# Remainders of expert rooms on column groups in plain fp32, a last room of 32 tokens with unsplit weights, and another order of the visits

## The chip, the cores and the metric

The kernel runs on one core of a Trainium2 chip. The metric is the device time of one execution in microseconds. The engines are TensorE (PE, whose weight loads the profile lists as PEld), VectorE (DVE), ScalarE (ACT), GpSimd (POOL) and SyncE (SP), which issues most of the DMAs.

## The reference

The inputs are q, k and v of 8 batches, 8 heads, 576 positions and 64 channels, and the weights of a router and of 8 experts. All is fp32.

```python
# attention: causal, a window of 128 positions, ALiBi bias
scores = where(0 <= i - j < 128, q @ k.T / 8 - slope[h] * abs(i - j), -1e9)
attn = softmax(scores) @ v                      # -> x: 8 x 576 tokens of 512

# routing: a token may keep the expert of the token before it
logits = x @ w_gate
local = sigmoid(x @ w_local)
e[s] = argmax(logits[s]) if s == 0 or local[s] < 0.5 else e[s - 1]

# expert: 512 -> 1024 -> 512
out[s] = softmax(logits[s])[e[s]] * (relu(x[s] @ w1[e[s]]) @ w2[e[s]])
```

Each of the 4608 tokens goes to one expert. With these inputs the eight experts get 418, 646, 542, 577, 610, 416, 616 and 783 tokens, which can be counted from the reference.

## The kernel before

**Attention.** A pair of heads of one batch is a slot, 32 in all. Every engine's work is put out in an order written by hand (`FIRST`, `ORDER`, `LAST`): `S` scores on PE, `D` bias and minimum on DVE, `E` exponential on ACT, `N` normalising on POOL, `U` transposes, `M` weighted values and so on. Ahead of the first slot the constants are made: `make_bias` writes, for each of four head pairs, four tiles of ALiBi bias (pairs 0 and 1 on DVE, 2 and 3 on POOL), and `zero` clears the unused corners of the probability tiles of both buffers. `tokens` computes the router's logits of a batch, with 32-column weights whose four results lie in four column groups of one PSUM tile. Attention's result goes to a DRAM table `xd` by blocks of tokens.

**Rooms.** The experts' work is laid out in rooms of a fixed number of 32-token blocks (`_plan`). Experts 0, 1 and 2 have own rooms of 256, 384 and 512 tokens. What is left over of all experts is ranked by size on the chip, and rank r gets the rooms `RANKS[r]`. The visits are, in tokens: own 256, 384, 512, then 512, 288, 384, 256, 384, 256, 384, 224, 448, 288, 192 and 128. A token that finds no room is left for a loop behind everything (L1207), one pass for each 128 such tokens of an expert; it isn't entered when there are none.

**A visit** (`Fixed.run`). Weights and activations are split into two fp32r parts, high and low, and each product takes three matmuls (`three`, L969 to L971). The first layer has 8 hidden blocks of 128: for each, 4 x 3 matmuls with the room's tokens as columns. ReLU on ACT (L1014) and the low part on DVE (L1015) follow. The second layer takes tokens in windows of 128 (`windows`): 3 matmuls of 512 columns for each window and hidden block. Where the room isn't a multiple of 128 tokens, the last window is moved back so that it overlaps the one before, at full price. `finish` scales each window by the gate (L976 on DVE, L978 on ACT), and `scatter` (L963, POOL) writes its 128 rows to the output. The last room, of 128 tokens, is a `Flex` visit: its tokens are the weights of the first layer and its hidden values are transposed on PE.

**Supply.** `Stream` loads the weights in chunks of 512 KB, eight for each visit (`load`, up to 6 chunks ahead of the splitting), and splits each in halves: high part on ACT (L237), low part on DVE (L239); up to 6 split chunks are held. `Feed` collects the next room's tokens: gathers on POOL (L177), one for 32 tokens, with one for the gates of a window, then for each window `split_x`: transpose on DVE (L183), high part on ACT (L186), low part on DVE (L187). `tick` is called at set places of a visit, and puts out at most one such turn, one gather and, at every third tick, one scatter. A turn of the next room may come as soon as a visit begins. Scatters that are left when the visits end are issued one behind another. All engines keep the order in which their instructions are put out.

## Time and profile before

| | us |
|---|---|
| median of 3 runs | 694.97 (694.80 to 695.07) |
| profiled execution | 696.09 |
| its span, first to last instruction | 694.2 |
| PE busy | 675.5 (97%) |
| DVE busy | 481.8 (69%) |
| ACT busy | 424.4 (61%) |
| POOL busy | 390.7 (56%) |

The span is the time from the first to the last instruction; the rest of the execution's time lies around it. A busy share is an average over stages: attention to some 240 us, then the visits. Matmuls are pipelined, so the time from the start of one to the start of the next tells more of PE's price than the length of one. A "granted clock" of 1.00 is 2.4 GHz, and the lower level is 1.2 GHz. Line L162 is that of a helper through which attention's instructions pass.

### The profile page before, as it was taken

How to read it: one execution, taken by the hardware profiler on the slowest of the kernel's cores; microseconds unless marked ns; L12 is line 12 of the kernel's file. 1: busy time of each engine (PE TensorE's matmuls, PEld its weight loads, DVE VectorE, ACT ScalarE, POOL GpSimd, SP SyncE). 2: the span in 40 equal slices, each digit the busy share in tenths (PEclk: the TensorE clock that was granted, in tenths of full speed). 3: DMA queues.
4: the chain of work that ended last, by engine and by line, in shares of the span. 5: the costliest groups of instructions: out<-in, count | busy, mean ns of one | idle time of the engine just before them, and what ended most of it. 6: DMA issues, size and time to landing. Idle time of an engine off the chain costs nothing. (4 is left out here: it accounts for less than half of the span.)

```text
span 694.2 us, 16083 instructions
## 1 busy us (share of the span) xinstructions
PE 675.5 (97%) x5339; PEld 550.9 (79%) x5339; DVE 481.8 (69%) x1649; ACT 424.4 (61%) x1200; POOL 390.7 (56%) x659
## 2 busy tenths in 40 slices
PE   8999999999999989999999999999999999999995
PEld 4667767767766677888888989899989878889894
DVE  7579889889898999964633664665576477345572
ACT  5999999999988653543523553564555355344462
POOL 6866656656787727777771737447466475102311
PEclk9999999999999999999999999999999999999999
DMA  9845655655822966445454655576576566345550
GB/s 299 249 138 175 222 156 174 223 156 172 265 65 60 294 201 206 126 161 163 141 162 126 209 181 165 177 232 207 152 239 200 148 197 219 104 132 173 173 158 30
DMA packets 61254, 121.99 MB, mean 176 GB/s; under 512 B 9391, under 2 KB 28335, under 8 KB 61168
## 3 DMA queue, kind: packets, MB, share of 16 engines
q1 hardware_dynamic: 51248, 100.12, 45.8%
q0 software_dynamic: 9488, 20.22, 9.5%
q8 instruction: 43, 0.70, 0.4%
q10 hardware_dynamic: 432, 0.59, 0.3%
q14 instruction: 43, 0.35, 0.2%
HBM read 101.29 MB, written 20.20 MB: 175 GB/s over the span
## 5 line engine op out<-in xcount | busy, mean ns | idle before, releaser
L239 DVE TENSOR_TENSOR cut<-wraw,cut 128x512 fp32r<-128x512 f32 x231 | 150.3, 688 | 53.6 <-ACT cut L237 52.4
L177 POOL DMA_INDIRECT kr<-xd,xidx x141 | 152.7, 1083 | 55.9 <-issue 38.7
L237 ACT CAST cut<-wraw 128x512 fp32r<-128x512 f32 x212 | 120.7, 618 | 56.3 <-PE y L971 56.1
L971 PE MATMUL h<-qx,cut 128*128 128x384 f32 (+6 forms) x440 | 142.1, 323 | 0.0
L970 PE MATMUL h<-qx,cut 128*128 128x384 f32 (+6 forms) x440 | 141.9, 322 | 0.0
L969 PE MATMUL h<-qx,cut 128*128 128x384 f32 (+6 forms) x440 | 141.6, 322 | 0.0
L969 PE MATMUL y<-cut,hh 128*128 128x512 f32 x328 | 129.6, 395 | 1.9 <-ACT hh L1014 1.1
L971 PE MATMUL y<-cut,hl 128*128 128x512 f32 x328 | 129.0, 395 | 1.5 <-DVE hl L1015 1.4
L963 POOL DMA_INDIRECT out<-y,sidx x41 | 43.2, 1053 | 153.1 <-ACT y L978 118.8
L970 PE MATMUL y<-cut,hh 128*128 128x512 f32 x328 | 129.3, 394 | 0.0
L1014 ACT ACTIVATE hh<-h 128x384 fp32r<-128x384 f32 (+6 forms) x104 | 47.8, 460 | 127.7 <-PE h L971 127.7
L162 POOL TENSOR_SCALAR cut<-cut,r 128x192 f32<-128x192 f32 (+2 forms) x256 | 99.6, 407 | 44.4 <-DVE r L162 14.8
L162 ACT ACTIVATE cut<-scs,mn 128x192 f32<-128x192 f32 (+2 forms) x256 | 108.9, 429 | 8.3 <-DVE mn L162 7.9
L1015 DVE SCALAR_TENSOR_TENSOR hl<-h,hh 128x384 fp32r<-128x384 f32 (+6 forms) x112 | 56.7, 507 | 81.4 <-ACT hh L1014 80.6
L969 PEld LDWEIGHTS h<-qx,cut 128*128 128x128 f32 x440 | 83.6, 190 | 6.6
L970 PEld LDWEIGHTS h<-qx,cut 128*128 128x128 f32 x440 | 83.7, 190 | 6.4 <-DVE qx L187 0.2
L162 DVE CUSTOM_DVE_ANT_0 scs<-sc,bias 128x192 f32<-128x192 f32 (+2 forms) x288 | 83.2, 324 | 7.3 <-PE sc L162 4.4
L971 PEld LDWEIGHTS h<-qx,cut 128*128 128x128 f32 x440 | 83.7, 190 | 3.4 <-issue 0.4
L971 PEld LDWEIGHTS y<-cut,hl 128*128 128x128 f32 x328 | 61.7, 188 | 16.1 <-DVE hl L1015 3.1
L969 PEld LDWEIGHTS y<-cut,hh 128*128 128x128 f32 x328 | 61.9, 189 | 13.2 <-ACT hh L162 1.8
L970 PEld LDWEIGHTS y<-cut,hh 128*128 128x128 f32 x328 | 61.9, 189 | 10.4 <-DVE cut L162 0.2
L162 PE MATMUL pt<-ident,cut 128*128 128x128 f32 x448 | 69.8, 281 | 0.4
(222 smaller groups left out, 1006.2 us busy)
## 6 DMA issues: line engine op xcount, KB each, us to landing
wraw<-w SPq DMA_DIRECT2D x120, 512.0 KB, 4.6
kr<-kT SPq DMA_DIRECT2D x31, 288.0 KB
qx<-qT SPq DMA_DIRECT2D x30, 288.0 KB, 4.6
cut<-v SPq DMA_DIRECT2D x8, 1024.0 KB
xd<-T SPq DMA_DIRECT2D x8, 768.0 KB
xd<-T SPq DMA_DIRECT2D x8, 384.0 KB
kr<-xd,xidx POOLq DMA_INDIRECT x141, 3.7
v<-v SPq DMA_DIRECT2D x8, 128.0 KB
```

The source lines that it names most:

```text
L162: ins = getattr(self.engine, name)(*args, **kw)
L177: queued(nc.gpsimd.indirect_dma_start(out=r, out_offset=None, in_=src[0:n, :], in_offset=bass.IndirectOffsetOnAxis(ap=col, axis=0), bounds ...
L237: scalar.copy(c[:, 0, f], raw[:, f])
L239: (pool if 2 * n + f == POOL_CUT else vector).tensor_tensor(c[:, 1, f], raw[:, f], c[:, 0, f], ALU.subtract)
L963: queued(nc.gpsimd.indirect_dma_start(out=out[:, :], out_offset=bass.IndirectOffsetOnAxis(ap=col, axis=0), in_=y, in_offset=None, bounds_c ...
L969: nc.tensor.matmul(o, ah, bh, start=start, stop=False)
L970: nc.tensor.matmul(o, ah, bl, start=False, stop=False)
L971: nc.tensor.matmul(o, al, bh, start=False, stop=stop)
L1014: now.act.activation(hh, hp, AF.Relu)
L1015: nc.vector.scalar_tensor_tensor(hl, hp, 0.0, hh, ALU.max, ALU.subtract)
```

## The change

- The fifth rank's room has 416 tokens (448), the last rank's 32 (128). The rooms are visited in another order: own 256, 384, 512, then 512, 288, 384, 416, 256, 288, 384, 192, 256, 384, 224 and 32.
- A room whose last window would have 32 or 64 tokens (288 twice, 416, 192) no longer moves it back. For these tokens ReLU writes fp32 values (`hx`), the raw chunks of the second layer are kept in pairs of tiles, and `rests` multiplies in plain fp32: the tokens are 32 or 64 columns of weights, and the 512 outputs are cut in four or two pieces, one for each column group. It is put out once for two hidden blocks. Index, gate and scatter follow: a row of the output is scattered in four or two pieces.
- The last room is a `Mini`: both layers in plain fp32 on four column groups, with weights that aren't split. Its first layer is put out ahead of the last hidden block's second layer of the room before, its two transposes in the middle of that, and its second layer behind it.
- In attention's start, half of bias 0 and all of bias 1 are made on ACT, and the clears for the second buffer follow the first slot's last score (`D6`).

```diff
-RANKS = [(512, 288), (384, 256), (384, 256), (384, 224), (448,), (288,), (192,), (128,)]
+RANKS = [(512, 288), (384, 256), (384, 256), (384, 224), (416,), (288,), (192,), (32,)]
+ORDER_OF_ROOMS = [0, 1, 2, 8, 3, 9, 4, 10, 5, 6, 7, 11]
...
-    return own + left
+    return own + [left[i] for i in ORDER_OF_ROOMS]
...
 def windows(nb):
-    return [min(4 * t, nb - 4) for t in range((nb + 3) // 4)]
+    last = nb % 4
+    if last in (1, 2):
+        return [(t, 4) for t in range(0, nb - last, 4)] + [(nb - last, last)]
+    return [(min(4 * t, nb - 4), 4) for t in range((nb + 3) // 4)]
...
+                e, which, c, kind = self.order[self.n_raw]
+                if kind and which == ("b" if kind == "also" else "a"):
+                    if c % 2 == 0:
+                        self.pair = tp.tile([P, 2, 2, DM], F32, name="xT")
+                    t = self.pair[:, c % 2]
+                else:
+                    t = wr.tile([P, 2, DM], F32, name="wraw")
+                self.raw.append(load_chunk(e() if callable(e) else e, which, c, t))
...
+                if self.order[self.n_cut][3] == "only":
+                    self.cut[self.n_cut] = self.raw.pop(0)
+                    self.n_cut += 1
+                else:
+                    run(self.split(self.room(), now.act, nc.vector))
...
-        order += [(e if kind == "own" else by_rank[e], w, c) for w, c in (FLEX_ORDER if nb == 4 else FIXED_ORDER)]
+        keep = "only" if nb == 1 else "also" if nb % 4 in (1, 2) else None
+        order += [(e if kind == "own" else by_rank[e], w, c, keep) for w, c in (FLEX_ORDER if nb == 1 else FIXED_ORDER)]
...
+        def make_bias(p, *engines):

             for turned in range(2):
+                engine = engines[turned % len(engines)]
                 for c in range(2):
                     at = slice(64 * c, 64 * c + 64)
-                    engine.tensor_scalar(bias[at, turned, p], rel[at], -8.0 * 2.0 ** -(2 * p + (c ^ turned) + 1), 1.0, ALU.mult, ALU.mult)
+                    slope = -8.0 * 2.0 ** -(2 * p + (c ^ turned) + 1)
+                    if engine is act:
+                        act.activation(bias[at, turned, p], rel[at], AF.Copy, scale=slope)
+                    else:
+                        engine.tensor_scalar(bias[at, turned, p], rel[at], slope, 1.0, ALU.mult, ALU.mult)
...
         zero(*zero_p(0))
-        make_bias(0, dve)
-        make_bias(1, dve)
-        zero(*zero_p(1), V[0][1][64:128])
+        make_bias(0, dve, act)
+        make_bias(1, act)
...
+            yield
+            dve.tensor_scalar(piece[:, 0:1], roff, 1.0 / 32, None, ALU.mult)
+            dve.tensor_scalar(piece[:, 1:2], roff, 64.0, None, ALU.is_ge)
...
+                w, r = wins[lo]
+                if r < 4:
+                    dve.tensor_tensor(fw[:, lo].rearrange("p (a q) -> p a q", q=r), t[:, w:w + r].unsqueeze(1).broadcast_to([P, 4 // r, r]),
+                                      msel.rearrange("p (a q) -> p a q", q=r), ALU.mult)
+                else:
+                    while hi < n and wins[hi] == (wins[hi - 1][0] + 4, 4):
+                        hi += 1
+                    dve.tensor_tensor(fw[:, lo:hi], t[:, w:w + 4 * (hi - lo)].rearrange("p (c q) -> p c q", q=4),
+                                      msel.unsqueeze(1).broadcast_to([P, hi - lo, 4]), ALU.mult)
...
+            for c, (w, r) in enumerate(wins):
+                if r < 4:
+                    col = sc[:, c0 + c:c0 + c + 1]
+                    dve.tensor_scalar(col, col, 4.0 / r, piece[:, r - 1:r], ALU.mult, ALU.add)
+                    yield
...
+                if emitted[-1] == ("D6", 0):
+                    zero(*zero_p(1), V[0][1][64:128])
...
-        queued(nc.gpsimd.indirect_dma_start(out=out[:, :], out_offset=bass.IndirectOffsetOnAxis(ap=col, axis=0), in_=y, in_offset=None,
-                                            bounds_check=NTOK - 1, oob_is_err=False))
+        n = DM // y.shape[1]
+        queued(nc.gpsimd.indirect_dma_start(out=out.rearrange("t (a c) -> (t a) c", a=n), out_offset=bass.IndirectOffsetOnAxis(ap=col, axis=0),
+                                            in_=y, in_offset=None, bounds_check=n * NTOK - 1, oob_is_err=False))
...
-        y = mp.tile([P, DM], F32, name="y", bufs=4)
+        y = mp.tile([P, DM], F32, name="y", bufs=4)[:, :o.shape[1]]
...
+        def run(self, W, tick, mini=None, ready=None):
             N = 32 * self.rows.blocks
-            wins = [slice(32 * w, 32 * w + P) for w in windows(self.rows.blocks)]
-            n = len(wins)
-            ys = [py.tile([P, DM], F32, name="y") for _ in range(n)]
+            wins = windows(self.rows.blocks)
+            n, rest = len(wins), wins[-1][1] % 4
+            M = N - 32 * rest
+            ys = [py.tile([P, DM], F32, name="y")[:, :P * r] for _, r in wins]
             xh, xl = self.rows.xh[:, :, :N], self.rows.xl[:, :, :N]
-            hs = {}
-
-            def second(f):
+            hs, hx = {}, None
+
+            def second(f, then=()):
                 hh, hl = hs.pop(f)
-                vh, vl = W.at("b")
-                for t, sl in enumerate(wins):
-                    three(ys[t], hh[:, sl], hl[:, sl], vh[:, f % 2], vl[:, f % 2], f == 0, f == 7)
+                vh, vl, raw = W.at("b")
+                for t, (w, r) in enumerate(wins):
+                    if r == 4:
+                        sl = slice(32 * w, 32 * w + P)
+                        three(ys[t], hh[:, sl], hl[:, sl], vh[:, f % 2], vl[:, f % 2], f == 0, f == 7)
+                    elif f % 2:
+                        rests(ys[t], lambda ff: hx[:, ff % 2], raw, (f - 1, f), r)
                     if t == n // 2 - 1:
                         tick()
+                        for g in then:
+                            g()
                 if f % 2:
                     W.done("b")
...
-                hh = mp.tile([P, N], F32R, name="hh", bufs=3)
-                hl = mp.tile([P, N], F32R, name="hl", bufs=3)
-                now.act.activation(hh, hp, AF.Relu)
-                nc.vector.scalar_tensor_tensor(hl, hp, 0.0, hh, ALU.max, ALU.subtract)
+                hh = mp.tile([P, M], F32R, name="hh", bufs=3)
+                hl = mp.tile([P, M], F32R, name="hl", bufs=3)
+                now.act.activation(hh, hp[:, :M], AF.Relu)
+                nc.vector.scalar_tensor_tensor(hl, hp[:, :M], 0.0, hh, ALU.max, ALU.subtract)
                 hs[f] = (hh, hl)
+                if rest:
+                    if f % 2 == 0:
+                        hx_next = mp.tile([P, 2, 32 * rest], F32, name="hx")
+                    now.act.activation(hx_next[:, f % 2], hp[:, M:], AF.Relu)
                 if f % 2:
                     W.done("a")
                 tick()
                 if f > 0:
                     second(f - 1)
+                if rest and f % 2:
+                    hx = hx_next
                 tick()
-            second(7)
+            if mini:
+                ready()
+                mini.first(W)
+            second(7, [mini.turn] if mini else ())
             for t in range(n):
                 c = self.rows.t0 + t
                 finish(ys[t], self.rows.g[:, t:t + 1], self.rows.idx[2][:, c:c + 1], t % 2)
+
+    def rests(y, h, raw, fs, r):
+
+        for f in fs:
+            for g in range(4 // r):
+                o = slice(32 * r * g, 32 * r * g + 32 * r)
+                nc.tensor.matmul(y[o], h(f), raw[:, f % 2, P * r * g:P * r * g + P * r], start=f == 0, stop=f == 7, skip_group_check=True)
+
+    class Mini(Fixed):
+
+
+        def first(self, W):
+            raws = [W.at("a") if i == 0 else W.cut[W.find("a") + i] for i in range(4)]
+            hp = ph_.tile([P, 256], F32, name="h")
+            for kc in range(4):
+                for g in range(4):
+                    nc.tensor.matmul(hp[32 * g:32 * g + 32], self.rows.x[:, kc], raws[g][:, :, P * kc:P * kc + P], start=kc == 0, stop=kc == 3,
+                                     skip_group_check=True)
+            for _ in range(4):
+                W.done("a")
+            self.h = mp.tile([P, 256], F32, name="hl", bufs=3)
+            now.act.activation(self.h, hp, AF.Relu)
+
+        def turn(self):
+            pt = ptr.tile([P, 2, P], F32, name="tr")
+            for i in range(2):
+                pin(nc.tensor.transpose(pt[:, i], self.h[:, P * i:P * i + P], ident))
+            self.hT = mp.tile([P, 2, P], F32, name="hh", bufs=3)
+            now.act.copy(self.hT, pt)
+
+        def run(self, W, tick, *_):
+            y = py.tile([P, P], F32, name="y")
+            for g in range(4):
+                rests(y, lambda f: self.hT[:, f % 2, 32 * g:32 * g + 32], W.at("b"), (2 * g, 2 * g + 1), 1)
+                W.done("b")
+            c = self.rows.t0
+            finish(y, self.rows.g[:, 0:1], self.rows.idx[2][:, c:c + 1], 0)
+
+    class MiniRows(Rows):
+        def turn(self, t):
+            self.x = sh.tile([P, KS, 32], F32, name="qx")
+            pin(nc.vector.transpose(self.x.rearrange("p c i -> p (c i)"), self.r[:, 0, 0]))

...
-            visits.append(Flex(xidx[:, x:x + 4], ridx[:, c:c + 1], sidx[:, c:c + 1]) if nb == 4 else Fixed(Rows(x, c, nb, idxs)))
+            visits.append(Mini(MiniRows(x, c, nb, idxs)) if nb == 1 else Fixed(Rows(x, c, nb, idxs)))
...
         if isinstance(v, Fixed):
-            upto = i + 1
-            while upto < len(visits) and isinstance(visits[upto], Flex):
-                upto += 1
-            v.run(W, lambda: feed.tick(upto))
-            feed.finish(upto)
-        else:
-            v.run(W, lambda: feed.tick(upto, False))
+            mini = visits[i + 1] if i + 2 == len(visits) else None
+            v.run(W, lambda: feed.tick(i + 1), mini, lambda: feed.finish(i + 1))
+            feed.finish(i + 1)
```

## Rows read from the trace of the kernel before

**Rows 1.** The page, part 1: busy us of each engine, share of the span, instructions.

```profile
PE 675.5 (97%) x5339; PEld 550.9 (79%) x5339; DVE 481.8 (69%) x1649; ACT 424.4 (61%) x1200; POOL 390.7 (56%) x659
```

**Rows 2.** The table of stretches, one for a visit: those of 512 (own), 288, 384, 256, 224, 448, 192 and 128 tokens. Columns: the stretch in us, its length, then busy us and instructions of PE, PEld, DVE, ACT and POOL, the granted clock of PE as a share of 2.4 GHz, the DMA engines' share and GB/s.

```profile
294.11:337.72 43.61, 43.61 (x193) 35.97 (x192) 24.00 (x41) 17.29 (x31) 33.85 (x33) 1.00 0.51 161
...
381.24:410.58 29.34, 29.34 (x169) 26.18 (x168) 18.70 (x32) 14.71 (x29) 15.23 (x16) 1.00 0.59 187
410.58:443.99 33.41, 33.41 (x170) 30.31 (x168) 17.78 (x30) 14.82 (x28) 20.31 (x20) 1.00 0.57 176
443.99:466.63 22.64, 22.64 (x146) 20.43 (x144) 17.20 (x31) 14.27 (x29) 11.65 (x11) 1.00 0.71 219
...
556.11:582.18 26.07, 24.41 (x145) 21.26 (x144) 17.92 (x33) 14.48 (x30) 17.82 (x16) 0.93 0.64 201
582.18:623.61 41.43, 41.43 (x193) 36.07 (x192) 19.32 (x32) 15.71 (x30) 9.18 (x9) 1.00 0.45 139
...
652.95:674.66 21.71, 21.71 (x146) 19.73 (x144) 14.37 (x27) 12.79 (x27) 7.44 (x7) 1.00 0.61 186
674.66:686.30 11.64, 11.64 (x80) 10.63 (x79) 5.96 (x11) 5.89 (x13) 2.51 (x2) 1.00 0.11 42
```

**Rows 3.** The timeline of all engines in the first 22 us, its lines on the bias and the first scores. Columns: start us, us, engine, line, operation, tiles, form, count; in brackets the idle time before it and what ended it.

```profile
2.19 1.28 ACT L162 ACT_TABLE_LOAD   x1 [2.19 <-issue]
...
3.36 2.66 DVE L162 TENSOR_SCALAR bias<-rel 64x192 f32<-64x192 f32 x7 [1.06 <-POOL rel L162]
...
4.58 1.31 PE L162 MATMUL sc<-kr,qx 64*64 64x64 f32 x16
...
7.45 0.22 DVE L162 CUSTOM_DVE_ANT_0 scs<-sc,bias 128x64 f32<-128x64 f32 x1
...
7.71 0.35 ACT L162 ACTIVATE cut<-scs,mn 128x64 f32<-128x64 f32 x1 [4.24 <-DVE mn L162]
...
8.44 0.44 ACT L162 ACTIVATE cut<-scs,mn 128x192 f32<-128x192 f32 x1
```

**Rows 4.** The timeline of POOL from 580 us on: one of the gathers, and scatters of the last rooms.

```profile
586.84 1.00 POOL L177 DMA_INDIRECT kr<-xd,xidx  x1 [0.30 <-issue]
...
622.74 1.02 POOL L963 DMA_INDIRECT out<-y,sidx  x1 [29.21 <-ACT y L978]
626.31 1.00 POOL L963 DMA_INDIRECT out<-y,sidx  x1 [2.55 <-DVE cut L239]
630.99 0.98 POOL L963 DMA_INDIRECT out<-y,sidx  x1 [3.68 <-issue]
...
675.14 1.00 POOL L963 DMA_INDIRECT out<-y,sidx  x1 [8.61 <-ACT y L978]
679.47 1.51 POOL L963 DMA_INDIRECT out<-y,sidx  x1 [3.33 <-DMA out<-y,sidx]
687.79 0.98 POOL L963 DMA_INDIRECT out<-y,sidx  x1 [6.82 <-ACTq L1207]
```

**Rows 5.** The timeline of PE between 39.5 and 46 us, in the attention phase: `pt` are transposes, `pk<-xT,w` the router logits on four column groups, `xa` the weighted values on two column groups.

```profile
39.74 1.09 PE L162 MATMUL pt<-ident,cut 128*128 128x128 f32 x8
40.77 1.07 PE L162 MATMUL pk<-xT,w 128*32 128x512 f32 x8
41.76 0.98 PE L162 MATMUL sc<-kr,qx 64*64 64x192 f32 x20
42.68 0.65 PE L162 MATMUL xa<-pts,cut 128*64 128x256 f32 x4
43.26 0.43 PE L162 MATMUL pk<-xT,w 128*32 128x128 f32 x8
43.62 0.44 PE L162 MATMUL pt<-ident,cut 128*128 128x128 f32 x2
...
44.11 0.60 PE L162 MATMUL pt<-ident,cut 128*128 128x128 f32 x4
44.55 0.60 PE L162 MATMUL pk<-ident,part 128*128 128x128 f32 x4
```

**Rows 6.** The timeline of ACT in the visit of 224 tokens.

```profile
560.23 0.62 ACT L186 CAST qx<-xtr 128x512 fp32r<-128x512 f32 x1 [1.42 <-DVE xtr L183]
562.36 0.62 ACT L186 CAST qx<-xtr 128x512 fp32r<-128x512 f32 x1 [1.50 <-DVE xtr L183]
562.88 0.35 ACT L1014 ACTIVATE hh<-h 128x224 fp32r<-128x224 f32 x1
```

**Rows 7.** The groups of DVE by shape between 244 and 300 us (count | busy us, mean ns): the table of tokens, and one of the index operations.

```profile
L858 DVE TENSOR_SCALAR cw<-io,at_t 128x128 f16<-128x128 f16 x40 | 7.3, 289 | 0.0
...
L162 DVE TENSOR_SCALAR xidx<-fi,roff 128x128 int32<-128x128 f32 x1 | 0.3, 274 | 0.0
```

**Rows 8.** The timeline of PE in the same visit.

```profile
561.88 0.27 PE L971 MATMUL h<-qx,cut 128*128 128x224 f32 x1
563.28 0.50 PE L969 MATMUL y<-cut,hh 128*128 128x512 f32 x1 [1.13 <-ACT hh L1014]
563.62 0.40 PE L970 MATMUL y<-cut,hh 128*128 128x512 f32 x1
564.51 0.50 PE L971 MATMUL y<-cut,hl 128*128 128x512 f32 x1 [0.49 <-DVE hl L1015]
...
565.95 0.41 PE L971 MATMUL h<-qx,cut 128*128 128x224 f32 x1
```

More of the change, by code (lines that the diff above doesn't have):

```diff
@@ L224, in at_once, with load_chunk @@
             r.turn(t)
[L226 removed]
+    def load_chunk(e, which, c, t):
         src = w1 if which == "a" else w2
[L228 removed]
         if isinstance(e, int):
@@ L250, in load @@
             while self.n_raw < len(self.order) and self.n_raw < self.n_cut + RAWS:
-                e, which, c = self.order[self.n_raw]
-                self.raw.append(load_chunk(e() if callable(e) else e, which, c))
+                e, which, c, kind = self.order[self.n_raw]
[6 more added lines that the diff above has]
+                self.raw.append(load_chunk(e() if callable(e) else e, which, c, t))
                 self.n_raw += 1
@@ L257, in fill @@
                 self.load()
-                run(self.split(self.room(), now.act, nc.vector))
+                if self.order[self.n_cut][3] == "only":
[3 more added lines that the diff above has]
+                    run(self.split(self.room(), now.act, nc.vector))
             self.load()
@@ L266, in split @@
             raw = self.raw.pop(0)
-            self.cut[self.n_cut] = c[:, 0], c[:, 1]
+            self.cut[self.n_cut] = c[:, 0], c[:, 1], raw
             self.n_cut += 1
@@ L921, in rank_tables @@
         yield from fill_table(trk, a_t, PACE_TABLE)
-        yield from indices(trk, idxs, XO[0], TO[0], [at + w for kind, _, at, nb in PLAN if kind == "rank" for w in windows(nb)])
+        yield from indices(trk, idxs, XO[0], TO[0], [(at + w, r) for kind, _, at, nb in PLAN if kind == "rank" for w, r in windows(nb)])
         rank_done.append(1)
@@ L1219, in moe_attention @@
         at_once(v)
-        v.run(Stream([(ev, w, c) for w, c in FLEX_ORDER]), lambda: None)
+        v.run(Stream([(ev, w, c, None) for w, c in FLEX_ORDER]), lambda: None)
         scatter(*pending.pop())
```

15 lines of the change are left out of this document (4 added, 11 removed).

## The prediction

> **What bounds the kernel now.** I read the page first: the tensor engine is busy for 97% of the span, 675.5 of 694.2 us, and no other engine passes 70% [rows 1]. Busy shares of PE are lengthened by the pipeline, so the next view is the table of stretches, one for each visit to a room [rows 2]. There PE is busy through the whole of every visit but one; DVE has 14 to 24 us of work and ACT 13 to 17 in visits of 22 to 44 us. A visit therefore lasts as long as its columns stream, and prices follow from the table. The visit of 512 tokens has 96 first-layer and 96 second-layer matmuls, all of 512 columns: 43.61 / 192 = 0.227 us. With 0.227 for a second-layer matmul (3 for each window and hidden block), the first-layer matmul comes out at 0.204 us for 448 columns ((41.43 - 96 x 0.227) / 96), 0.178 for 384, 0.135 for 288, 0.122 for 256 and 0.113 for 192. The one visit with idle time on PE is that of 224 tokens: 24.41 of 26.07 us busy, clock 0.93.
>
> Two stretches are not bound by PE. At the start everything waits for DVE to make its constants [rows 3]. At the end three scatters run one after another [rows 4].
>
> **The rooms with a remainder.** Four rooms lose a window of the second layer: 288 tokens twice, 416 (was 448) and 192. A window is 3 matmuls for each of 8 hidden blocks: 24 x 0.227 = 5.45 us each. In its place, every second hidden block, stand plain fp32 matmuls on column groups. The kernel before has that very form: 32-column weights, four outputs in four column groups [rows 5]. Each fp32 matmul appears there twice (x8 for four), so I count two rounds for a group of four. Four of 512 columns take 41.76 - 40.77 = 0.99 us to the next start, four of 128 columns 43.62 - 43.26 = 0.36. The difference, 0.63 for 2 rounds of 384 more columns, is 0.105 us for a round of 128: the four groups stream together, or it would be four times that. The fixed part is 0.36 - 0.21 = 0.15 us, which includes leaving the mode; entering it costs another 0.15 (eight transposes ahead of it take 1.03, where four elsewhere take 0.44).
>
> With a remainder of 32, two hidden blocks take 4 rounds: 0.42 + 0.15 + 0.15 = 0.72 us, four times a room: 2.9. Bounds: 0.42 if the fixed parts hide, 0.87 if each group of four pays its 0.36 and the entry. I take 0.72, nearest to the row, with one entry and one exit. With a remainder of 64 there are two column groups and 256 columns; the nearest row is xa on 64-column weights: 0.58 us for two rounds with the exit, so 0.215 a round and 4 x 0.215 + 0.30 = 1.16 us, 4.6 a room (bounds 0.86 and 1.31). All of this is PE time on the path:
> - 288 tokens, twice: 2 x (-5.45 + 2.88) = -5.1
> - 416 tokens: -5.45 + 2.88, and 96 first-layer matmuls with 32 columns fewer, 0.191 for 0.204 (midway between the prices at 448 and 384): -1.3; together -3.9
> - 192 tokens: -5.45 + 4.64 = -0.8
>
> That is -9.8 us. The extra ReLU on ACT, eight in such a room, costs nothing: ACT has 14.7 of 29.3 us of work there [rows 2], and its reader comes after one or more windows of 0.68 us; uncovered, each is bounded by the 0.35 us of a 224-column ReLU [rows 6]. The raw chunks that are kept occupy two tiles, which the next room with a remainder asks for 16 chunks later, past the 12 chunks by which SP runs ahead, so SP isn't held. The extra index operations are a few DVE operations of up to 0.3 us [rows 7] in a visit where DVE works 24.0 of 43.6 us [rows 2].
>
> **The order of the visits.** No matmul is added or removed by it, and each room's eight loads and its gathers go with it. What changes is the neighbour. In the visit of 224 tokens the next room's four windows (448 tokens) are turned in its first two hidden blocks: three full ones and a half one, each a step on DVE, one on ACT (0.6 us) and one more on DVE, with ACT waiting 1.4 to 1.5 us for DVE before two of them [rows 6]. The ReLU stands behind these on ACT, so PE stops for 1.4 us from 561.88 and 0.9 from 563.62, and then it runs at the lower clock for a while: the same matmul lasts 0.41 us in place of 0.27 [rows 8], and the granted clock is 0.93 over the visit, between its levels of 1.2 and 2.4 GHz [rows 2]. A visit of 224 without this is 96 x 0.1175 (midway between 192 and 256) + 10.9 = 22.2 us, so 3.9 are lost. After the change this room's neighbour is the 32-token room, with one small transpose. Late next would be the other short rooms: before 288 (two windows and a 32-token one), 256 (two) and 384 (three). The visit of 256 at 444 us had three windows to turn and no idle PE (22.64 of 22.64). So -3.9, between 0 and -3.9.
>
> **The start.** Before, DVE makes eight pieces of bias (to 6.0 us) and clears ten tiles ahead of its first score at 7.45, so the clears take up to 1.4 us; the scores were on PE from 4.58 [rows 3]. Now it makes two pieces; ACT makes six, from the end of its table load at 3.47, at no more than the 0.44 of its 128x192 operation: to 6.1. The first exponential moves from 7.71 to about 6.1, and ACT is dense from there. The clears move behind the first pair's last score, where ACT has exponentials in hand. I take -1.5; bounds -2.4 (first score half a us after PE starts on them) and +1.4 (no gain, and the clears uncovered).
>
> **The end.** The last visit took PE 11.6 us, from 674.66 to 686.3 [rows 2]. The new one has a first part of 8 rounds of 256 columns, 8 x 0.215 + 0.3 = 2.0 us, and two transposes, 0.2, both ahead of the end of the 224-token room, then a second part of 16 rounds of 128: 2.0. On PE alone 11.6 become 4.2. But the room's two scatters and the last one are issued together at the end, and each waits for the landing of the one before: 675.14 to 679.47 is 4.33 us with a wait on that DMA, and three in a row stood 3.57 and 4.68 apart [rows 4]. Counted from the end of the last room's old position, the first scatter comes at 2.2 + 0.48 + 0.38 (the copy that ACT makes first) = 3.1, the third 8.7 later at 11.7, and the end 6.4 after that (687.79 to 694.2): 18.1 for 19.5, so -1.4. With spacings of 3.57 or 4.68: -2.9 or -0.7.
>
> **The sum.** -9.8 - 3.9 - 1.5 - 1.4 = -16.6 us. The profiled execution took 696.09 (span 694.2 and 1.9 around it), so 679.5; it lay 1.1 above the median of 694.97, and the forecast for the median is 678.4.
>
> **Rivals.**
> 1. The idle time moves to another short visit. For it: visits of 21 to 23 us have 14 to 17 us on DVE [rows 2], and the 192-token room now lasts some 20.9. Against: none has four windows to turn. Time: 678.4 + 3.9 = 682.3.
> 2. The start gives nothing, since a later wait swallows it: 679.9, or 681.3 with the clears uncovered.
> 3. The column groups overlap less beside these neighbours. By the row's upper bound (0.87 and 1.31) the rooms take 2.4 more and the last room's first part 0.5: 681.3. The Trainium skill, "TensorE: Matmul & The Clock Gate", Part 3 ("Measured speedup vs the span model"), gives 2.38 for three column tiles; an estimate by it stretches the streaming by 3 / 2.38, about 2.7 us more in all, 681.1. The trace leans against it: the 0.105 us of a round already holds all four groups [rows 5].
> 4. The scatters at the end don't wait for each other: the end follows PE, 2.2 + 2.0 + 1.5 (686.3 to 687.79) + 6.4 = 12.1 for 19.5, and the time is 672.4. Against: the waits of [rows 4].
> 5. Slower: the column groups run one after another. It decides where a pair of hidden blocks takes over 1.36 us in place of 0.72, for then a 288-token room gains nothing. Wholly serial, a pair takes 16 x 0.105 + 0.3 = 1.98 (+15.1 over twelve), with 64 tokens 2.02 (+3.4), and the last room's first part 7.2 (+5.2): 702.1. Against: the 0.36 of four groups [rows 5].
> 6. Slower: a room overflows. Counted from the reference's inputs, the fifth rank has 416 tokens for 416 places, the last 30 for 32. One token more in either starts a pass of the loop behind everything: a table of 7.3 us on DVE [rows 7], five gathers of 1.0 and a scatter's landing and wait of 4.3 [rows 4], 11.6 of PE [rows 2] and the 6.4 of the end once more at most, 28 to 35: about 710.
>
> **How the numbers follow.** Chances: forecast 0.49, idle time moved 0.20, start 0.10, less overlap 0.10, free scatters 0.06, overflow 0.03, serial groups 0.02. The likeliest case's own range is 674 to 682. For 8 in 10 I take 671.5 (rival 4, or the fixed parts hidden: 12 x 0.30 + 4 x 0.30 = 4.8 less) to 685 (rivals 1 and 3 together: 685.2). A change under 0.2%, 1.4 us, couldn't be told from none. Rivals 5 and 6 end slower: 0.05; within 0.2% needs most of the parts to fail at once: 0.01.
>
> **What would show it.** The groups of fp32 matmuls: about 0.72 us of PE for a pair of hidden blocks, visits of 288 at 26.8 us, of 416 at 37.6, of 192 at 20.9. The 224-token visit at about 22.2 us, apart from the last room's first part, with the clock at 1.00 throughout. The first exponential near 6.1 us and the first own room's matmuls 1.5 us earlier. At the end three scatters over 4 us apart with PE long finished. The prediction is wrong if PE idles in a visit to a short room, if a pair takes over 1 us, or if the branch into the loop is taken.

## The result, and the profile after

The changed kernel takes 679.12 us in the median (678.48 to 679.92) against 694.88 for the kernel before on the same chip: a ratio of 0.9774 (95% interval 0.9757 to 0.9791). The forecast was 678.4. The profiled execution took 678.48, with a span of 676.8, so 17.4 us less span than before where the sum said 16.6.

Busy time by engine, page part 1 of the kernel after, to lay beside [rows 1]:

```profile
PE 656.5 (97%) x5485; PEld 528.0 (78%) x5485; DVE 466.0 (69%) x1637; ACT 418.1 (62%) x1217; POOL 392.6 (58%) x655
```

PE has more instructions and is busy 19 us less, at the same share: it is still the bound. The table of stretches after, columns as in [rows 2]: the own visit of 512, then 288 (the second such visit takes the same 26.68), 416, 192, 224 (up to the last room's first part), and what is left of PE's work.

```profile
293.34:337.49 44.15, 43.93 (x193) 36.06 (x193) 25.04 (x45) 17.60 (x31) 33.48 (x33) 1.00 0.58 185
381.01:407.69 26.68, 26.68 (x209) 22.72 (x207) 18.23 (x32) 15.85 (x38) 20.58 (x21) 1.00 0.60 198
...
441.21:478.49 37.28, 37.28 (x233) 32.49 (x231) 18.00 (x30) 16.56 (x37) 15.16 (x14) 1.00 0.47 152
...
561.33:582.89 21.56, 21.54 (x154) 16.69 (x152) 15.45 (x30) 14.36 (x37) 17.29 (x15) 1.00 0.64 203
...
638.96:659.48 20.52, 20.52 (x139) 18.45 (x137) 7.44 (x16) 6.65 (x15) 3.19 (x3) 1.00 0.26 88
659.48:665.30 5.82, 5.70 (x105) 3.84 (x104) 0.75 (x1) 1.33 (x3) 0.98 (x1) 1.00 0.09 34
```

Against [rows 2], stage by stage:

| stage | forecast | measured in the two profiles |
|---|---|---|
| start, as it stands through attention | -1.5 | -0.74 |
| own visit of 512 | 0 | +0.54 (43.61 to 44.15) |
| 288, each | -2.6 | -2.66 (29.34 to 26.68) |
| 416 for 448 | -3.9 | -4.15 (41.43 to 37.28) |
| 192 | -0.8 | -0.15 (21.71 to 21.56) |
| 224 and all behind it | -5.3 | -7.74 (45.58 to 37.84) |

That is -17.6; the other visits give 0.2 back. Two terms are well off, one at each end of the kernel, with opposite signs.

The timeline of ACT and DVE at the start, for [rows 3]:

```profile
3.49 2.25 ACT L167 ACTIVATE bias<-rel 64x192 f32<-64x192 f32 x6
...
5.76 0.35 ACT L167 ACTIVATE cut<-scs,mn 128x64 f32<-128x64 f32 x1
...
8.56 0.63 DVE L167 MEMSET cut<- 128x64 f32 x8
...
9.41 0.48 DVE L167 MEMSET v<- 64x512 f32 x1
...
10.54 0.35 ACT L167 ACTIVATE cut<-scs,mn 128x64 f32<-128x64 f32 x1 [0.71 <-DVE mn L167]
```

The first exponential is 1.95 us earlier (7.71 to 5.76), more than forecast. Then the moved clears occupy DVE from 8.56 to 9.9, the next slot's scores come behind them, and ACT idles 0.71 us for the minimum they yield. From there on attention runs 0.74 us ahead of before.

PE's timeline shows a pair of hidden blocks in the first 288-token visit, then one in the 192-token visit, for [rows 5]:

```profile
388.29 0.39 PE L1006 MATMUL y<-cut,hl 128*128 128x512 f32 x1
388.61 0.65 PE L1084 MATMUL y<-xT,hx 128*32 128x128 f32 x16
389.18 0.40 PE L1004 MATMUL h<-qx,cut 128*128 128x288 f32 x1
389.42 0.29 PE L1005 MATMUL h<-qx,cut 128*128 128x288 f32 x1
...
567.37 1.08 PE L1084 MATMUL y<-xT,hx 128*64 128x256 f32 x8
568.39 0.36 PE L1004 MATMUL h<-qx,cut 128*128 128x192 f32 x1
```

From start to start the 16 matmuls take 0.57 us, entering costs 0.09 (0.32 where 0.23 is usual) and leaving 0.11 (0.24 for 0.13): 0.77. By the length of the visit it is (26.68 - 29.34 + 5.45) / 4 = 0.70; the forecast was 0.72. With 64 tokens the matmuls take 1.02.

At the start of the own visit of 512 the same view has a stop of PE that before didn't have: it waits for the low part of the visit's last turn (the last window of its tokens that is transposed and split).

```profile
293.33 0.73 PE L1004 MATMUL h<-qx,cut 128*128 128x512 f32 x2
294.29 0.50 PE L1005 MATMUL h<-qx,cut 128*128 128x512 f32 x1 [0.22 <-DVE qx L192]
```

POOL's timeline at the end, for [rows 4]:

```profile
663.31 0.98 POOL L998 DMA_INDIRECT out<-y,sidx  x1 [14.54 <-ACT hh L1106]
667.23 0.98 POOL L998 DMA_INDIRECT out<-y,sidx  x1 [2.94 <-issue]
670.60 0.98 POOL L998 DMA_INDIRECT out<-y,sidx  x1 [2.39 <-issue]
```

PE's work is over at 665.3; three scatters stand 3.92 and 3.37 us apart and the span ends 6.2 behind the last. Before, PE's last matmul ended at 686.8 and its scatter went out at 687.79 [rows 4]: the end has passed from PE to the scatters. What the last two wait for the profile doesn't name here ("issue"); b3 below looks at it.

### The profile page after: what moved, and what is told of

It reads as the page before. It is cut to its first block, busy times and chain, and to the rows that moved or that the text cites. A ratio compares the mean times of both kernels' runs of the same rounds, so it can differ in the third digit from the quotient of the medians.

```text
span 676.8 us, 16362 instructions
## 1 busy us (share of the span) xinstructions
PE 656.5 (97%) x5485; PEld 528.0 (78%) x5485; DVE 466.0 (69%) x1637; ACT 418.1 (62%) x1217; POOL 392.6 (58%) x655
## 5 line engine op out<-in xcount | busy, mean ns | idle before, releaser
L182 POOL DMA_INDIRECT kr<-xd,xidx x141 | 155.3, 1101 | 55.3 <-issue 39.4
L243 DVE TENSOR_TENSOR cut<-wraw,cut 128x512 fp32r<-128x512 f32 x183 | 118.8, 687 | 30.0 <-ACT cut L241 28.6
L1056 ACT ACTIVATE hh<-h 128x384 fp32r<-128x384 f32 (+4 forms) x104 | 46.6, 448 | 132.9 <-PE h L1006 131.2
L1057 DVE SCALAR_TENSOR_TENSOR hl<-h,hh 128x256 fp32r<-128x256 f32 (+4 forms) x112 | 55.4, 496 | 88.4 <-ACT hh L1056 88.0
L1004 PE MATMUL y<-cut,hh 128*128 128x512 f32 x288 | 113.7, 395 | 0.8 <-ACT hh L167 0.8
L1006 PE MATMUL y<-cut,hl 128*128 128x512 f32 x288 | 113.1, 394 | 0.9 <-DVE hl L1057 0.9
L1005 PE MATMUL y<-cut,hh 128*128 128x512 f32 x288 | 113.3, 393 | 0.0
L241 ACT CAST cut<-wraw 128x512 fp32r<-128x512 f32 x164 | 93.6, 618 | 24.6 <-PE y L1006 23.9
L1006 PEld LDWEIGHTS y<-cut,hl 128*128 128x128 f32 x288 | 54.0, 188 | 13.5 <-DVE hl L1057 2.1
L167 PE MATMUL sc<-kr,qx 64*64 64x192 f32 (+2 forms) x1152 | 61.9, 319 | 1.2 <-DVE mn L167 1.2
L1004 PEld LDWEIGHTS y<-cut,hh 128*128 128x128 f32 x288 | 54.2, 188 | 10.7 <-ACT hh L167 1.8
```

Of the source, the lines that this page charges most:

```text
L167: ins = getattr(self.engine, name)(*args, **kw)
L182: queued(nc.gpsimd.indirect_dma_start(out=r, out_offset=None, in_=src[0:n, :], in_offset=bass.IndirectOffsetOnAxis(ap=col, axis=0), bounds ...
L241: scalar.copy(c[:, 0, f], raw[:, f])
L243: (pool if 2 * n + f == POOL_CUT else vector).tensor_tensor(c[:, 1, f], raw[:, f], c[:, 0, f], ALU.subtract)
L1004: nc.tensor.matmul(o, ah, bh, start=start, stop=False)
L1005: nc.tensor.matmul(o, ah, bl, start=False, stop=False)
```

## The experiments

The kernel before, run beside them on the same chip, had medians of 695.22 (a1 to a4), 696.87 (b1, b2, d1, d3) and 696.61 us (b3, c1 to c3), so between these groups ratios are compared. An interval of a ratio is 1 to 1.7 us wide on either side; effects below that are read from the stages of the profiles. One idle time differs between the profiles: at 247 us PE loses 0.95 us in those of before and after, and 1.58 in those of a1, a3, a4, b1, c3 and d3. As a3, a4 and b1 change nothing that is executed ahead of it, I put it down to no edit.

### The start

**a1, the old start.** The first slots' bias and clears as before:

```diff
-        make_bias(0, dve, act)
-        make_bias(1, act)
+        make_bias(0, dve)
+        make_bias(1, dve)
+        zero(*zero_p(1), V[0][1][64:128])
...
-                if emitted[-1] == ("D6", 0):
-                    zero(*zero_p(1), V[0][1][64:128])
```

> The changed kernel with the start of the kernel before: bias 0 and 1 on DVE, and the second buffer's clears ahead of the first score. Theory: in the changed kernel the clears are uncovered, so of the 2.0 us by which the first exponential came earlier only 0.7 was kept; the time is 0.7 us above the changed kernel's 679.1, 679.8, with the own room of 384 tokens starting near 256.0 us. Rival, the forecast's term: the start is worth 1.5, so 680.6. Rival: a later wait swallows all of it, 679.1.

Measured: 680.91 us, ratio 0.9793 (0.9779 to 0.9808). Attention runs 0.74 us later than in after, what it had gained. Another 0.63 is the wait at 247 us, which is the long one here; whether the old start has a part in that isn't shown. By the stages the start is worth 0.74, half of its term.

**a2, the clears on POOL.** The same start, with the clears neither on DVE nor behind the scores:

```diff
         make_bias(3, pool)
+        for a in (*zero_p(1), V[0][1][64:128]):
+            pool.memset(a, 0.0)
...
-                if emitted[-1] == ("D6", 0):
-                    zero(*zero_p(1), V[0][1][64:128])
```

> The changed kernel with the second buffer's clears on POOL, behind its bias of pairs 2 and 3, in place of DVE behind the first slot's last score. Theory: those 1.3 us of DVE sit on the path of the second slot, so its first score moves from 10.0 to about 8.7 us and the kernel takes 1.3 us less: 677.8. Rival: PE or ACT is the bound there already, so the second slot gains less than 0.3 us: 678.8 to 679.1.

Measured: 678.65 us, ratio 0.9758 (0.9742 to 0.9773). Attention gains 0.64 us over after, about half of the clears' 1.3. The timelines of POOL and DVE show what is late next:

```profile
8.97 0.20 POOL L167 TENSOR_SCALAR r<-sm 128x4 f32<-128x4 f32 x1
...
9.20 0.18 DVE L167 RECIPROCAL r<-r 128x4 f32<-128x4 f32 x1 [0.46 <-POOL r L167]
...
9.48 1.48 POOL L167 TENSOR_SCALAR cut<-cut,r 128x64 f32<-128x64 f32 x4 [0.31 <-DVE r L167]
```

The next slot's first exponential no longer waits. But POOL's own step for the first slot's reciprocal is now behind the clears (8.97 us, 7.59 in after), and DVE waits 0.46 us for it. The normalising that follows begins at 9.48, where in after it is

```profile
10.20 1.47 POOL L167 TENSOR_SCALAR cut<-cut,r 128x64 f32<-128x64 f32 x4 [2.42 <-DVE r L167]
```

That is 0.72 us earlier and not 1.3. So the clears on DVE had a price, and on POOL half of it stays, one step on.

### The remainders

**a3, no remainders on column groups.** The windows of 288, 416 and 192 are moved back again, in split form, at the new sizes and in the new order:

```diff
-    if last in (1, 2):
+    if nb == 1:
...
-        keep = "only" if nb == 1 else "also" if nb % 4 in (1, 2) else None
+        keep = "only" if nb == 1 else None
```

> The changed kernel with the remainders of 32 and 64 tokens computed by a full window of 128 again (moved back over the one before), all else as changed. Theory: a pair of hidden blocks on column groups costs 0.8 us (32 tokens) or 1.3 us (64) where six matmuls of 512 columns cost 1.37; the visits of 288 go from 26.7 to 29.3 us, that of 416 from 37.3 to about 40.2, that of 192 from 21.6 to 21.7, together 8.3 us more: 687.4. Rival: part of what the column groups saved is given back in waits elsewhere, so that undoing them costs less than 6 us: below 685.

Measured: 687.97 us, ratio 0.9892 (0.9874 to 0.991), 0.0118 above after: 8.2 us. The stretch of the first 288-token visit is that of before again; that of 192 is longer than before:

```profile
382.16:411.50 29.34, 29.34 (x170) 26.18 (x168) 18.73 (x32) 14.70 (x29) 22.42 (x23) 1.00 0.62 194
...
570.23:592.46 22.23, 22.20 (x145) 19.74 (x144) 15.45 (x29) 13.31 (x28) 17.66 (x16) 1.00 0.74 235
```

The forecast's rooms without the first layer's 1.3 come to 8.5. Confirmed in place and size. The room of 192 tokens takes 22.23 us here and in b1 (the new order alone, below), and took 21.71 before: so its remainder saves 0.67 (22.23 to 21.56, forecast 0.8), and the new order costs it 0.52. In its first hidden block PE's weight load, in after, waits for a low part, which is behind a turn of the next room on DVE:

```profile
564.75 0.19 PEld L1006 LDWEIGHTS y<-cut,hl 128*128 128x128 f32 x1 [0.45 <-DVE hl L1057]
```

**c1, one hidden block at a time.** The remainder's matmuls in groups of half the size, twice as many entries and exits:

```diff
...
-                    elif f % 2:
-                        rests(ys[t], lambda ff: hx[:, ff % 2], raw, (f - 1, f), r)
+                    else:
+                        rests(ys[t], lambda ff: hxs[ff][:, ff % 2], raw, (f,), r)
...
```

> The changed kernel with the remainder's matmuls issued for every hidden block by itself, so 16 more entries into and exits from the plain fp32 groups and no other work. Theory: entry and exit together cost 0.30 to 0.37 us (a pair measured 0.79 in after, 0.42 of it the streaming): 4.8 to 5.9 us more, 684.0 to 685.0. Rival: the fixed part belongs to the streaming of the groups and not to the change of form: under 1 us more, 679.1 to 680.1.

Measured: 685.78 us, ratio 0.9845 (0.9823 to 0.9867), 5.9 above c2, which ran beside it. The 288-token visits take 28.05 us, 1.37 more for four more groups: 0.34 each. PE's timeline:

```profile
389.26 0.43 PE L1085 MATMUL y<-xT,hx 128*32 128x128 f32 x8
389.62 0.40 PE L1004 MATMUL h<-qx,cut 128*128 128x288 f32 x1
```

Eight matmuls take 0.36, where sixteen take 0.57: 0.21 for eight more (the streaming), 0.15 fixed, and entry and exit besides. It is the division that the forecast read from [rows 5], and putting out two hidden blocks at once saves some 5.5 us.

**c2, the groups outside.** The two blocks of one column group in succession, then the next group:

```diff
-        for f in fs:
-            for g in range(4 // r):
+        for g in range(4 // r):
+            for f in fs:
```

> The changed kernel with the two loops of a pair exchanged: the two hidden blocks of one column group follow each other, then the next group. The same instructions, another order. Theory: column groups overlap only with neighbours on other groups, so two matmuls in a row on one group wait for each other: of eight slots of 0.21 us five remain one after another where two did, 0.63 us more for each of twelve pairs of 32 tokens and some 0.4 for each of four of 64, 9 us more, 688 (686 to 690). Rival: TensorE holds the groups apart whatever the order: 679.1. A second rival, wholly serial groups: about 700.

Measured: 679.93 us, ratio 0.9761 (0.974 to 0.9782), the same as after. My theory of 688 falls. PE's timeline:

```profile
388.45 0.67 PE L1084 MATMUL y<-xT,hx 128*32 128x128 f32 x16
389.05 0.40 PE L1004 MATMUL h<-qx,cut 128*128 128x288 f32 x1
```

The sixteen take 0.60 in place of 0.57. Neighbours on the same column group don't hold each other up by more than 0.03 us in a pair.

### The order of the visits

**a4, the old order** with every other edit:

```diff
-ORDER_OF_ROOMS = [0, 1, 2, 8, 3, 9, 4, 10, 5, 6, 7, 11]
+ORDER_OF_ROOMS = list(range(12))
```

> The changed kernel with its rooms in the order of their ranks, so that the 224-token room stands before the 416-token one again, whose three full windows and 32 tokens are turned in its visit. Theory: the neighbour makes the idle time; PE stops in the visit of 224 tokens again and the clock falls, 2 to 4 us: 681 to 683. Rival: the idle time came from the fourth window's size (64 tokens then, 32 now) or by chance: no idle PE in that visit and 679.1.

Measured: 694.72 us, ratio 0.9994 (0.9981 to 1.0006): 15 us lost, where I expected 2 to 4 (the profiled execution was a long one, 697.38). The idle time in the 224-token visit is back (24.31 us for it, 1.5 of them idle), but that is the small part. The stretches of 288, of 192 (up to the last room's first part) and of the last room, which now follow 416 directly:

```profile
615.68:644.52 28.84, 27.45 (x212) 22.59 (x208) 16.00 (x30) 14.46 (x36) 5.19 (x6) 1.00 0.52 176
644.52:670.50 25.98, 23.01 (x145) 17.93 (x141) 6.61 (x16) 7.14 (x22) 3.14 (x3) 0.87 0.39 123
670.50:688.00 17.50, 11.45 (x110) 5.88 (x109) 0.54 (x2) 1.67 (x4) 1.97 (x2) 0.63 0.55 200
```

The first had 26.68 in after; the other two are divided otherwise there, and take 19.41 and 5.95 in d1 below, which has this order too. The granted clock falls to 0.87 and 0.63 here, between its two levels. The waits of SP from 575 us on, and of all engines from 636 (total, times, longest):

```profile
SPq L236 <- PE y L1084: 85.6, 6, 22.8
...
PE h L1094 <- DMA xT<-w: 5.1, 2, 4.4
...
ACT cut L241 <- DMA xT<-w: 4.5, 2, 3.9
```

SP, which loads the weights in order, waits for PE's remainder matmuls (L1084), up to 22.8 us at a time: a load into a pair tile has to wait until the room ahead has read it, and every later load stands behind. New theory: two pair tiles are too few for rooms with remainders in succession.

**d1, the old order with a third pair tile** (two small tiles elsewhere share the places of others, to make room):

```diff
...
-                        self.pair = tp.tile([P, 2, 2, DM], F32, name="xT")
+                        n = sum(bool(kind) and c % 2 == 0 and which == ("b" if kind == "also" else "a") for _, which, c, kind in self.order[:self.n_raw])
+                        self.pair = (tp.tile([P, 2, 2, DM], F32, name="xT") if n % 3 < 2
+                                     else mp.tile([P, 2, 2, DM], F32, name="pair", bufs=1))
...
```

> The changed kernel with the rooms in the old order, and a third pair tile for the raw chunks of the rooms with a remainder (taken every third time from a tile of its own; the Flex loop's row tile and the routing's hold tile share others to make the place). Theory: what the old order lost (694.7 against 679.1) is SP's queue held at the pair tiles: the rooms of 416, 288, 192 and 32 tokens follow one another there, and each asks for both tiles while the room ahead still reads them. With a third tile SP can run some 12 chunks ahead again, and all but the idle time in the 224-token visit (about 2 us in that run) comes back: 681 to 683 us. Rival: the four short rooms use up weights faster than SP's queue lands them, wherever they go: 692 to 695.

Measured: 680.43 us, ratio 0.9768 (0.9745 to 0.9792). The stretches of 224, 288, 192 and the last room, and SP's waits on the remainders:

```profile
553.41:579.33 25.92, 24.40 (x145) 21.26 (x144) 17.64 (x33) 14.37 (x30) 17.12 (x16) 0.93 0.71 242
...
616.63:643.43 26.80, 26.80 (x213) 22.83 (x209) 16.35 (x30) 15.02 (x37) 5.17 (x6) 1.00 0.50 170
643.43:662.84 19.41, 19.41 (x145) 15.80 (x141) 6.61 (x16) 6.66 (x22) 2.77 (x3) 1.00 0.59 194
662.84:668.79 5.95, 5.95 (x110) 3.87 (x109) 0.54 (x2) 1.56 (x4) 0.98 (x1) 1.00 0.53 210
```

```profile
SPq L236 <- PE y L1086: 69.6, 5, 22.8
```

One tile more, and the loss is gone, all in the three rooms; the rival (weights used up faster than they land) falls. SP's longest wait is the same 22.8 us: a long wait in a loading queue says nothing by itself. What counts is how far the queue was ahead when it began. The 224-token visit is as slow as it was before, with its clock at 0.93.

**d3, the new order with the same third tile**, as the control; its edit is d1's without the order.

> The changed kernel in its own order with the same third pair tile. Theory: in this order the rooms with a remainder never follow one another but at 192 and the last, so the two tiles are free in time: 678.7 to 679.5, no change. Rival: the two tiles hold SP in this order too: 1 us or more faster.

Measured: 679.99 us, ratio 0.9759 (0.9738 to 0.978): no change from after that can be told. So in the new order two tiles are enough, as the prediction said. Beside d1 the order itself is worth 0.4 us by medians and 2.3 by the two profiled spans (679.8 and 677.5). d1's executions spread from 679.54 to 682.39, so I leave it between these.

**b1, the new order alone**, in the kernel before:

```diff
-    return own + left
+    return own + [left[i] for i in [0, 1, 2, 8, 3, 9, 4, 10, 5, 6, 7, 11]]
```

> The kernel before with the visits in the new order and nothing else. The forecast's step: the idle time in the 224-token visit goes and nothing takes its place: 3.9 us less, 691.1 (690.5 to 691.7). Rival: as the old order shows only some 2 us idle in that visit when the other edits are made, part of the 3.9 us is cost that the new neighbour has as well: 692.5 to 693.5. A second rival: the order costs or gains nothing without the remainders' pair tiles: 694.5 to 695.5.

Measured: 692.85 us, ratio 0.9948 (0.9929 to 0.9967), so 3.6 us less (2.3 to 4.9). The own visit of 512 and the visit of 224:

```profile
294.49:338.55 44.06, 44.06 (x193) 35.99 (x193) 24.26 (x42) 17.20 (x31) 34.30 (x33) 1.00 0.53 163
...
649.62:671.44 21.82, 21.82 (x145) 19.77 (x144) 14.67 (x27) 13.04 (x27) 7.49 (x7) 1.00 0.59 186
```

The visit of 224 takes 21.82 for 26.07, without idle time and at a clock of 1.00: the forecast's mechanism, 4.25 for its 3.9. But the own visit of 512 takes 0.45 longer, as it does in after, and that of 192 takes 0.52 longer (a3): 3.3 remain, near the measured 3.6.

The 0.45 comes from the index operations for all rooms, which are put out ahead of the own visit of 512, in the own visit of 384. They are merged over windows that follow each other in the table, and the new order breaks these runs: 13 multiplications on DVE where the kernel before has 6, and 14 after the whole change. A stretch of that visit in the kernel before (columns as in [rows 2]), and the multiplications on DVE's timeline, before and in b1:

```profile
280.00:290.00 10.00, 10.00 (x58) 8.63 (x58) 9.18 (x36) 4.19 (x8) 7.23 (x8) 1.00 0.42 127
...
289.27 0.62 DVE L162 TENSOR_TENSOR fi<-trk,msel 128x24 f32<-128x24 f32 x6
```

```profile
289.47 1.11 DVE L162 TENSOR_TENSOR fi<-trk,msel 128x24 f32<-128x24 f32 x13
```

DVE is busy for 9.18 of 10 us there, and the multiplications take 0.49 us more (1.19, so 0.57 more, in after). The last turn of the next visit stands behind them, and its low part is what PE waits for at 294 us in after. c3 below moves them. The order has a price in other visits than its gain.

### The end

**b2, the old last room** at the end of the changed kernel:

```diff
-RANKS = [(512, 288), (384, 256), (384, 256), (384, 224), (416,), (288,), (192,), (32,)]
+RANKS = [(512, 288), (384, 256), (384, 256), (384, 224), (416,), (288,), (192,), (128,)]
...
-            visits.append(Mini(MiniRows(x, c, nb, idxs)) if nb == 1 else Fixed(Rows(x, c, nb, idxs)))
+            visits.append(Flex(xidx[:, x:x + 4], ridx[:, c:c + 1], sidx[:, c:c + 1]) if nb == 4 else Fixed(Rows(x, c, nb, idxs)))
...
```

> The changed kernel with the last room as before: 128 tokens, split weights, its own turn and two transposes. Theory: the 224-token visit and all behind it took 7.7 us less than before, 3.9 of them the idle time of that visit, so the end itself gave some 3.8 us: 683.0 (682.3 to 683.7). Rival, the forecast's own term: 1.4 us, since the scatters end last either way: 680.5 (680.1 to 681.0). If instead TensorE's work of the last room set the end, 7 us: 686.

Measured: 682.89 us, ratio 0.9801 (0.978 to 0.9822), 2.9 above d3, which ran beside it. From the start of the 224-token visit to the end it is 41.0 us (640.07 to 681.1) against 37.84: 3.2. POOL's last scatters:

```profile
665.86 0.99 POOL L998 DMA_INDIRECT out<-y,sidx  x1 [2.51 <-DVE cut L243]
674.89 0.98 POOL L998 DMA_INDIRECT out<-y,sidx  x1 [8.04 <-ACTq L1300]
```

With the old room the last scatter follows PE (8.04 us of waiting), not the scatter ahead.

**b3, one scatter more.** The last room's scatter is issued twice, with the same rows and data:

```diff
             finish(y, self.rows.g[:, 0:1], self.rows.idx[2][:, c:c + 1], 0)
+            pending.append(pending[-1])
```

> The changed kernel with the last room's scatter issued twice (the same rows, the same data). Theory: behind the last rooms the scatters follow one another at the pace of their landing (3.92 and 3.37 us apart in the profile of after) and these, no longer TensorE, set the end: one more adds 3.4 to 3.9 us, 682.5 to 683.0. Rival: the spacing is only the issue on POOL (1.0 us each and some 0.3 between): 680.4. Without effect, 679.1, if the end is set by something else.

Measured: 681.69 us, ratio 0.9792 (0.977 to 0.9815), 1.8 above c2, which ran beside it. With intervals of 1.5 us on either side the times alone don't tell this from the rival's 1.3; the profiled execution does:

```profile
667.62 0.98 POOL L998 DMA_INDIRECT out<-y,sidx  x1 [2.89 <-issue]
670.99 0.97 POOL L998 DMA_INDIRECT out<-y,sidx  x1 [2.39 <-issue]
673.48 0.97 POOL L998 DMA_INDIRECT out<-y,sidx  x1 [1.51 <-DMA out<-y,sidx]
```

The chain theory holds in kind: the added scatter goes out 2.49 us behind the one before, 1.51 of them in a wait for that one's DMA, and the span ends 2.8 later than in after, 0.4 of which was there ahead of the first scatter (663.75 for 663.31). For the two scatters ahead of it the profile names no wait ("issue"), so there the landing is argued, from this row and [rows 4]. The spacing is 2.49 and not 3.4. What differs is the scatter waited for: the first two write 256 KB each, the last room's 64 KB. By the Trainium skill, "DMA: Bandwidth & Descriptors", section "Anatomy of one DMA — SWDGE (gpsimd) path", a DMA issued from GpSimd takes 2.0 us and its bytes over 436 GB/s, which makes an estimate of 2.60 and 2.15. The measured spacings of 3.37 and 2.49 fall with the size too, by more, and lie above it.

### A version that could have been faster

**c3** puts the clears on POOL, visits the room of 32 ahead of 224, and spreads the index operations:

```diff
-ORDER_OF_ROOMS = [0, 1, 2, 8, 3, 9, 4, 10, 5, 6, 7, 11]
+ORDER_OF_ROOMS = [0, 1, 2, 8, 3, 9, 4, 10, 5, 6, 11, 7]
...
                 lo = hi
+                if lo % 8 < 2:
+                    yield
...
-            mini = visits[i + 1] if i + 2 == len(visits) else None
-            v.run(W, lambda: feed.tick(i + 1), mini, lambda: feed.finish(i + 1))
-            feed.finish(i + 1)
+            mini = visits[i + 1] if i + 1 < len(visits) and isinstance(visits[i + 1], Mini) else None
+            v.run(W, lambda: feed.tick(i + 1), mini, lambda: feed.finish(i + 1))
+            feed.finish(i + 2 if mini else i + 1)
```

> The changed kernel with three edits: the clears on POOL (0.5 us as measured), the room of 32 tokens visited ahead of that of 224, so that two scatters in place of three stand behind the last matmul, and the index operations of the tables spread over more ticks, for the 0.55 us that the own visit of 512 tokens grew. Theory: PE then ends 224 tokens at about the time it ended the last room, the second scatter comes 3.4 to 3.9 us after the first, and the end is 1.4 us earlier; with the 0.5 and the 0.5 it is 676.7 (676.2 to 677.3). Rival: the room of 384, which then hosts the small room's first part and turns both next rooms, gets idle time or the scatter chain of that room runs into the last: 678 to 679.5, no better than the clears alone.

Measured: 682.62 us, ratio 0.9799 (0.9774 to 0.9824): 2.7 us slower than c2, which ran beside it. The own visit of 512, the passage over the small room, and the visit of 224:

```profile
293.29:336.81 43.52, 43.52 (x194) 36.04 (x192) 25.02 (x49) 17.71 (x32) 33.26 (x32) 1.00 0.57 184
...
636.34:645.80 9.46, 6.55 (x109) 4.34 (x108) 6.33 (x11) 6.22 (x13) 1.03 (x1) 0.98 0.73 233
645.80:671.30 25.50, 25.40 (x144) 22.52 (x144) 6.43 (x14) 5.89 (x14) 3.06 (x3) 0.87 0.11 41
```

With the index operations spread, the last turn's transposition stands ahead of the last of them (289.17 us, 291.49 in after), and the own visit of 512 gives 0.63 us back (43.52 for 44.15), though there are 15 multiplications for 14: it was their place (c3's other edits put nothing into this stretch). But the rooms' turns aren't put out while the small room is worked on, so the 224-token room's come all at once behind it; PE idles 2.9 us (9.46 less 6.55), and then the clock is at 0.87 in the next visit, 25.5 us long. The rival named this place; it was dearer than it said.

## Why the prediction was right

The forecast's path was the one that was taken: PE the bound, rooms and idle time the two large terms, scatters at the end. It was 0.7 us off in the median, which is in part luck: terms at either end of the kernel were missed with opposite signs. Step by step:

- **The rooms: right.** -9.8 forecast, -9.6 measured, a pair at 0.70 to 0.77 for 0.72; a3 shows that the edit carries it and c1 that the fixed part was read rightly from [rows 5]. Rival 3 falls. The estimate by the Trainium skill's 2.38 for three column tiles ("TensorE: Matmul & The Clock Gate", Part 3, "Measured speedup vs the span model") would make a 288-token visit 29.34 - 5.45 + 4 x 0.83 = 27.2; it took 26.68. The 192-token room missed its term by 0.65, and the greater part isn't the remainder's: PE's second-layer matmuls of its first hidden block stand 0.34, 0.41 and 0.34 apart for 0.23, some 0.4 us, as they do in a3 without the remainder. That is the new order (a3: 0.52).
- **The order: the term right, the step incomplete.** The idle time in the 224-token visit went (b1, 4.25 for 3.9). Rival 1 came true in small: 0.5 us in the 192-token visit, and nothing more. "What changes is the neighbour" held for the turns only. The order also changes who is next to whom at the pair tiles, worth 15 us with two tiles (a4 beside d1), and how the index operations merge. The sentence that SP isn't held since the tiles are asked for again 16 chunks later is right for the new order (d3) and depends wholly on it.
- **The index operations, put at nothing: wrong.** "In a visit where DVE works 24.0 of 43.6 us" is the wrong row: they are put out one visit ahead, in the own visit of 384, where DVE is busy for 9.18 of 10 us, and the next visit's last turn stands behind them. It came to 0.54 us, of which the order alone gives 0.45 (b1). c3 gives it back by spreading them.
- **The start: mis-sized, -0.74 for -1.5.** The step that failed is that the clears lie "where ACT has exponentials in hand". ACT had none left for 0.71 us. Rival 2, in which a later wait takes it all, is half true.
- **The end: mis-sized, -3.2 (b2) to -3.5 for -1.4.** The mechanism held: PE finishes early and three scatters set the end. The spacing was taken as 4.33 twice, 8.7; it was 3.92 and 3.37, 7.3. The lower bound of 3.57 gave -2.9. The first scatter also came 0.6 earlier than worked out, counted from 660.78 (638.96 and b2's 21.82): 2.5 for 3.1. Rival 4 falls: b3's last scatter waits for the one before.

The misses are +0.54, +0.76 and +0.65 on one side and -2.4 on the other (the end with the idle time), so the sum is nearer than its terms.

## What to carry to other kernels

When work is put in another order, follow each buffer that is reused and ask how many uses apart its users are: two tiles were enough only because no two rooms that need them are neighbours, and an order that seemed worth 4 us held off a loss of 15. A long wait of a loading queue isn't yet a loss; look for the engine that then waits for the data. A step "hidden" by an average share has to be laid against the timeline at the very place where it is put out: here that was one visit ahead of the row that was read.

## What the runs showed of the hardware

Sixteen fp32 matmuls on four column groups start in four rounds some 0.11 us apart, in whichever order the groups are put out (c2); the records don't name the group, so how the engine arranges it isn't shown. Each change between these and the other form costs 0.34 us for entry, exit and the fixed part together (c1). And idle time on PE can cost twice: beside its longest waits the granted clock of a stretch lies between the two levels. It is 0.87 behind a wait of 2.61 us in c3, 0.87 in the stretch with a wait of 2.88 and 0.63 in that with one of 4.36 in a4, and 0.93 in that with one of 1.12 in d1. It isn't so each time: the 224-token visit of a4 has that same 1.12 and stays at 1.00. In after, where the profile lists no wait of PE behind 300 us, it is 1.00 in every stretch shown.
